# Output tiles summed in pairs from one pool of six PSUM banks, in place of groups of four from a pool of four banks

## The chip, the cores and the metric

The kernel runs on one core of one Trainium2 chip. The metric is the device time of one execution in microseconds (us); the median of several runs counts. The engines are named as in the profile: PE is TensorE (matmuls), PEld its weight loads, DVE is VectorE, ACT is ScalarE, POOL is GpSimd and SP is SyncE. A name with a q, such as SPq or ACTq, means what that engine issues for DMA.

## The reference, cut to what matters

One input `x` of 2048 tokens by 512 goes through two branches. Branch A is linear attention with 32 heads of 16, whose feature map is two softmaxes. Branch B is a gated MLP whose gate is mixed over the tokens. A sigmoid of `x` weighs the two.

```python
x = A_x
g = _sigmoid((x * gate_w).sum(-1, keepdims=True))
# branch A
qkv = (x @ wqkv).reshape(B, S, 3, H, Dh).transpose(2, 0, 3, 1, 4)
pq = einsum('bhsd,hdf->bhsf', q, w_phi)          # the same for k
phi_q = concatenate([softmax(pq), softmax(-pq)])  # the same for k
kv = einsum('bhsf,bhsd->bhfd', phi_k, v)
num = einsum('bhqf,bhfd->bhqd', phi_q, kv)
den = einsum('bhqf,bhf->bhq', phi_q, phi_k.sum(s)) + 1e-06
a = (num / den) @ wo
# branch B
z = gelu(x @ w_in)                       # 2048 x 1376
z1 = z[..., :688]
z2 = layernorm(z[..., 688:])
gate = einsum('ts,bsf->btf', w_sp, z2) + b_sp
b = (z1 * gate) @ w_out
return g * a + (1 - g) * b
```

## The kernel before

The 2048 tokens are 16 tiles of 128. The work has three stages.

The first stage (to about 46 us in the profile) computes `z1` and `z2` for all tiles (L188) and folds the feature weights into the projections of q and k (L308).

The second stage goes through the 16 tiles for the keys and values: `k_tile` and `v_tile` multiply a tile with its weights, and `kv_acc` sums the products in the PSUM tile `kvacc`. In between it already takes work of the third stage: `gg_next` calls `gg_half`, which makes one half of a tile's mixed gate with 16 matmuls of 128 by 344 (L449), and DVE turns the result into `ucat` (L454). After a tile's second half `u_T` has SP issue a DMA transpose of `ucat` into `uT` (L480). 16 of the 32 halves are done when this stage ends at about 120 us. `q_tile` (L357 for the matmuls, two exponentials on ACT at L361, then DVE, POOL and a DMA transpose into `eqT` at L391) has by then been called for six tiles.

The third stage, which the change is about, is the loop at L573. Three kinds of work alternate on PE:

- `attn_tile(i)`: eight small matmuls into the PSUM tile `at` (L462), which has one buffer; DVE makes `rden` and `o` of them (L465, L467), and SP issues the transpose of `o` into `oT` (L475).
- `q_tile(i + 6)` and `gg_next()`, as above.
- the output: `ba_main` sums nine matmuls of 128 by 512 for one tile, four with `oT` (L486) and five with `uT` (L488); `ba_rem` adds the last 48 rows of the 688 (L491); `ba_store` scales the sum on ACT into `ob` (L502) and ACT issues the store (L503). `ob` has two buffers.

The rows of `ba_rem` lie in the lower or the upper 64 partitions, depending on whether the tile is even or odd. `ba_step` sums one tile at each step of the loop and keeps the sums of a group of four (`BA_GROUPS`; the last group has two) in PSUM. At the group's last tile it does the four `ba_rem` matmuls one behind the other, and then the four stores. Tiles 14 and 15 are done by `ba_tile` at the end, with `ba_rem` over all 128 partitions; tile 15 is cut into columns 0 to 384 and 384 to 512, and the second piece goes out through DVE and SP (L498, L500).

PSUM has eight banks. `kvacc` and later `at` take two (tag `kvat`). In the second stage the other six are the pool `psK`. Ahead of the loop `psK` is closed and its six banks become `psG` with two buffers (for `q_tile` and `gg_half`) and `psC` with four (for the output sums).

The order of PE and ACT is the program's order (`manual_schedule`); DVE, POOL and SP are put in order by the scheduler. Each engine works its queue in order.

Of the kernel before, what the change touches and what calls it, by code (L numbers as in the profile page):

```python
# [10 lines left out]
FP32 = mybir.dt.float32  # L11
BF16 = mybir.dt.bfloat16
I32 = mybir.dt.int32

P = 128
S = 2048
D = 512
# [5 lines left out]
NT = S // P  # L23
NDT = D // P
CH = 512
NCH = S // CH
NFT = (FH + P - 1) // P
FPAD = NFT * P
NG = 4
# [6 lines left out]
def kernel(  # L36
# [43 lines left out]
    halves = [slice(64 * h, 64 * h + 64) for h in range(2)]  # L80
# [238 lines left out]
    with tc.manual_schedule(engines={mybir.EngineType.PE, mybir.EngineType.Activation}):  # L319
# [22 lines left out]
    early_cm.__exit__(None, None, None)  # L342
    psM = ctx.enter_context(
        tc.tile_pool(name="psM", bufs=1, space=bass.MemoryType.PSUM, reuse_waits="tile"))
    psK_cm = tc.tile_pool(name="psK", bufs=6, space=bass.MemoryType.PSUM, reuse_waits="tile")
    mm_pool = psK_cm.__enter__()
    work = ctx.enter_context(tc.tile_pool(name="work", bufs=2, reuse_waits="tile"))
    kvp_cm = tc.tile_pool(name="kvp", bufs=2, side="right", reuse_waits="tile")
    kvp = kvp_cm.__enter__()

    def mm_tile():
        return mm_pool.tile([P, CH], FP32, name="mm")

    def expo(pool, name, bufs, tt, w):
        ps = mm_tile()
        for dt in range(NDT):
            nc.tensor.matmul(ps[:, :], lhsT=xT[:, dt, tt * P:(tt + 1) * P], rhs=w[:, dt, :],  # L357
                             start=(dt == 0), stop=(dt == NDT - 1))
        e = pool.tile([P, H, 2, DH], BF16, name=name, bufs=bufs)
        for a in range(2):  # L360
            nc.scalar.activation(  # L361
                out=e[:, :, a, :], in_=ps[:, :].rearrange("p (h f) -> p h f", f=DH),
                func=AF.Exp, scale=1.0 - 2.0 * a)
        z = work.tile([P, H, 2], FP32, name="zs")
        nc.vector.tensor_reduce(  # L365
            out=z[:].rearrange("p h a -> p (h a)"), in_=e[:].rearrange("p h a f -> p (h a) f"),
            axis=AX.X, op=ALU.add,
        )
        return e, z

    def even_out(e, z, rz):
        ratio = work.tile([P, H], FP32, name="ratio")
        nc.vector.tensor_tensor(out=ratio[:], in0=z[:, :, 0], in1=rz, op=ALU.mult)  # L373
        nc.gpsimd.tensor_tensor(  # L374
            out=e[:, :, 1, :], in0=e[:, :, 1, :],
            in1=ratio[:, :, None].to_broadcast([P, H, DH]), op=ALU.mult)
# [8 lines left out]
    def q_tile(tt):  # L385
        eq, z = expo(work, "eq", 3, tt, wq_p)
        rq = work.tile([P, H], FP32, name="rq")
        nc.vector.reciprocal(out=rq[:], in_=z[:, :, 1])
        even_out(eq, z, rq[:])
        eqT = work.tile([P, 8, P], BF16, name="eqT", bufs=7)  # L390
        nc.sync.dma_start_transpose(out=eqT[:, :, :], in_=eq[:].rearrange("p h a f -> p (h a f)"))  # L391
        eqTs[tt] = eqT

# [65 lines left out]
    def attn_tile(tt):  # L459
        at = psM.tile([P, 8, P], FP32, name="at", tag="kvat", bufs=1)  # L460
        for g in range(8):
            nc.tensor.matmul(  # L462
                at[:, g, 0:AW], lhsT=eqTs[tt][:, g, :], rhs=kvz[:, g, :], start=True, stop=True)
        rden = work.tile([P, 8, NG], FP32, name="rden")
        nc.vector.reciprocal(out=rden[:], in_=at[:, :, 64:AW])  # L465
        o = work.tile([P, D], BF16, name="o")
        nc.vector.scalar_tensor_tensor(  # L467
            out=o[:].rearrange("p (u h d) -> p u h d", u=8, d=DH),
            in0=at[:, :, 0:64].rearrange("p u (h d) -> p u h d", d=DH),
            scalar=g_el[:, tt:tt + 1],  # L470
            in1=rden[:, :, :, None].to_broadcast([P, 8, NG, DH]),
            op0=ALU.mult, op1=ALU.mult,
        )
        oT = work.tile([P, NG, P], BF16, name="oT", bufs=5)
        nc.sync.dma_start_transpose(out=oT[:, :, :], in_=o[:, :])  # L475
        oTs[tt] = oT

    def u_T(tt):
        uT = work.tile([P, NFT, P], BF16, name="uT", bufs=11)
        nc.sync.dma_start_transpose(out=uT[:, :, :], in_=ucat[tt % NU][:, :])  # L480
        return uT

    def ba_main(acc, tt, c0=0, c1=D):
        oT, uT, i = oTs[tt], uTs[tt], tt % 2
        for g in range(NG):
            nc.tensor.matmul(acc, lhsT=oT[:, g, :], rhs=wo_t[:, g, c0:c1], start=(g == 0), stop=False)  # L486
        for ft in range(5):
            nc.tensor.matmul(acc, lhsT=uT[:, i + ft, :], rhs=w_main[i][:, ft, c0:c1], start=False, stop=False)  # L488

    def ba_rem(acc, tt, rows, c0=0, c1=D):  # L490
        nc.tensor.matmul(  # L491
            acc, lhsT=uTs[tt][rows, 5 * (1 - tt % 2), :], rhs=w_rem[rows, c0:c1], start=False, stop=True)

    def ba_store(acc, tt, c0, c1, on_dve):
        ob = work.tile([P, c1 - c0], BF16, name=f"ob{c1 - c0}")
        dst = out2[tt * P:(tt + 1) * P, c0:c1]
        if on_dve:
            nc.vector.tensor_scalar(  # L498
                out=ob[:, :], in0=acc, scalar1=g_inv[:, tt:tt + 1], scalar2=None, op0=ALU.mult)
            nc.sync.dma_start(out=dst, in_=ob[:, :])  # L500
        else:
            nc.scalar.activation(out=ob[:, :], in_=acc, func=AF.Copy, scale=g_inv[:, tt:tt + 1])  # L502
            nc.scalar.dma_start(out=dst, in_=ob[:, :])  # L503

    def acc_tile():
        return psC.tile([P, CH], FP32, name="acc")

    def ba_tile(tt, cuts=(0, D)):
        for h, (c0, c1) in enumerate(zip(cuts, cuts[1:])):
            acc = acc_tile()[:, 0:c1 - c0]  # L510
            ba_main(acc, tt, c0, c1)
            ba_rem(acc, tt, slice(0, P), c0, c1)
            ba_store(acc, tt, c0, c1, h > 0)

    def ba_step(tt):
        group = next(g for g in BA_GROUPS if tt in g)
        accs[tt] = acc_tile()
        ba_main(accs[tt][:, :], tt)
        if tt == group[-1]:
            for t in group:  # L520
                ba_rem(accs[t][:, :], t, halves[t % 2])
            for t in group:
                ba_store(accs[t][:, :], t, 0, D, False)

    oTs = {}
    uTs = {}
    eqTs = {}
    accs = {}
    BA_GROUPS = [range(0, 4), range(4, 8), range(8, 12), range(12, 14)]
    Q_AT = (5, 7, 9, 11, 13, 15)  # L530
    ggs = [(tt, j) for tt in range(NT) for j in range(2)]

    def gg_next():
        tt, j = ggs.pop(0)
        gg_half(tt, j)
        if j == 1:
            uTs[tt] = u_T(tt)

    with tc.manual_schedule(engines={mybir.EngineType.PE, mybir.EngineType.Activation}):
        ks = {0: k_tile(0)}  # L540
        kvacc = psM.tile([P, 8, P], FP32, name="kvacc", tag="kvat", bufs=1)
        pend = []
        for tt in range(NT):
            if tt + 1 < NT:
                ks[tt + 1] = k_tile(tt + 1)
            ek, rk = ks.pop(tt)
            pend.append((tt, ek, v_tile(tt, rk)))
            if len(pend) == 3:
                kv_acc(*pend.pop(0))
            if tt > 0:  # L550
                gg_next()
            if tt in Q_AT:
                q_tile(Q_AT.index(tt))
        nc.scalar.activation(out=g_el[:, :], in_=glog[:, :], func=AF.Exp)
        nc.vector.tensor_scalar(out=g_1p[:, :], in0=g_el[:, :], scalar1=1.0, scalar2=None, op0=ALU.add)
        nc.vector.reciprocal(out=g_inv[:, :], in_=g_1p[:, :])
        for p_ in pend:
            kv_acc(*p_)
        kvz_evac()
        kvp_cm.__exit__(None, None, None)  # L560
        kvw_cm.__exit__(None, None, None)
        outw = ctx.enter_context(
            tc.tile_pool(name="outw", bufs=1, side="right", reuse_waits="tile"))
        gg_next()
        w_main, w_rem, wo_t = load_out_weights()
        nq = len(Q_AT)
        psK_cm.__exit__(None, None, None)
        mm_pool = ctx.enter_context(
            tc.tile_pool(name="psG", bufs=2, space=bass.MemoryType.PSUM, reuse_waits="tile"))
        psC = ctx.enter_context(  # L570
            tc.tile_pool(name="psC", bufs=4, space=bass.MemoryType.PSUM, reuse_waits="tile"))
        attn_tile(0)
        for i in range(NT - 1):  # L573
            if i + nq < NT:
                q_tile(i + nq)
            gg_next()
            attn_tile(i + 1)
            if i == 0:
                gg_next()
            elif i < NT - 1:  # L580
                ba_step(i - 1)
        ba_tile(14)
        ba_tile(15, cuts=(0, 384, D))


# [28 lines left out]
```

## Time and profile before

| What | Value |
|---|---|
| median of 3 runs | 210.19 us (210.04 to 210.28) |
| the profiled execution | 210.28 us |
| its span, first to last instruction | 208.6 us |
| mean granted clock of PE | 0.997 |
| DVE busy | 131.2 us (63%) |
| ACT busy | 75.0 us (36%) |
| POOL busy | 47.0 us (23%) |
| L449, the halves of the gate | 512 matmuls, 79.9 us busy |
| L488 and L486, the output sums | 85 and 61 matmuls recorded, 20.1 and 15.6 us busy |
| L502, the stores' scaling on ACT | 16 instructions, 10.9 us busy |
| transposes into uT: issue to landing | 2.7 / 2.8 / 6.4 us (min, median, max of 16) |
| transposes into oT: issue to landing | 2.4 / 2.5 / 5.3 us (of 16) |

A matmul's duration in a row reaches from its start to its modelled end and overlaps the next one's, so what a run of matmuls costs is read from start to start: 16 of L449 take 2.33 us, four of L357 or L486 0.86 us, five of L488 1.08 us, eight of L462 0.26 us. Some matmul records are missing, which is why a count can be one too low.

### The profile page before, as it was taken

What the parts mean: (1) busy time and instruction counts of PE and PEld (TensorE: products, weight loads), DVE (VectorE), ACT (ScalarE), POOL (GpSimd) and SP (SyncE); (2) the same over time, 40 slices, a digit from 0 to 9 for tenths busy, and PEclk for the clock granted to TensorE, in tenths of its full rate; (3) what the DMA queues carried; (4) which work ended last, traced back from release to release, by engine and by line L of the source; (5) the groups of instructions that cost most, each with busy time, mean ns of one, the idle gap of its engine ahead of it and who ended that gap; (6) DMA issues with size and microseconds to landing.
All of it is one profiled execution on the core that took longest, in us unless ns stands there. A gap on an engine that the chain in (4) does not pass through costs nothing.

```text
span 208.6 us, 3745 instructions
## 1 busy us (share of the span) xinstructions
PE 202.5 (97%) x1432; PEld 121.5 (58%) x1449; DVE 131.2 (63%) x282; ACT 75.0 (36%) x121; POOL 47.0 (23%) x79
## 2 busy tenths in 40 slices
PE   8899999999999999999999999999999999999994
PEld 3566667665656565655556656555455555665642
DVE  2477786764996787979788667555448553443330
ACT  3566666668223423232323222222251123302322
POOL 8020202020544242424252322222204220110000
PEclk9999999999999999999999999999999999999998
DMA  6999999999920404224040599854562558264342
GB/s 187 269 219 211 216 286 155 269 270 207 290 58 0 42 2 88 51 40 83 9 88 0 97 339 164 152 91 88 106 157 57 111 107 137 75 113 89 105 113 75
DMA packets 88994, 27.20 MB, mean 130 GB/s; under 512 B 82992, under 2 KB 88976, under 8 KB 88976
## 3 DMA queue, kind: packets, MB, share of 16 engines
q1 hardware_dynamic: 83680, 22.42, 56.1%
q10 hardware_dynamic: 5232, 4.54, 7.4%
q8 instruction: 11, 0.18, 0.3%
q14 instruction: 7, 0.06, 0.1%
q0 software_dynamic: 64, 0.01, 0.0%
HBM read 4.41 MB, written 2.10 MB: 31 GB/s over the span
## 4 chain that ended last, share of the span: by engine, by line
PE 91%; DMA 4%; ACT 2%; issue 1%; DVE 0%; SPq 0%; ACTq 0%
PE mm L449 35%; PE zp L188 18%; PE mm L357 12%; PE acc L488 8%; PE mm L397 7%; PE acc L486 6%; DMA w_z<-in_B_w_in_dram 2%; PE kvacc L413 2%; PE at L462 2%; DMA out_dram<-ob 1%; PE acc L491 1%; ACT ob L502 1%; PE fps L308 1%; ACT eq L361 1%; ACTq L503 0%
## 5 line engine op out<-in xcount | busy, mean ns | idle before, releaser
L449 PE MATMUL mm<-z2all,wspT 128*128 128x344 bf16 x512 | 79.9, 309 | 0.6 <-DVE ucat L454 0.4
L449 PEld LDWEIGHTS <-wspT 128*128 128x128 bf16 x512 | 49.0, 98 | 26.3 <-issue 1.4
L188 PE MATMUL zp<-w_z,xT 128*128 128x344 bf16 (+1 forms) x256 | 40.2, 311 | 0.5 <-DMA w_z<-in_B_w_in_dram 0.3
L361 ACT ACTIVATE eq<-mm 128x512 bf16<-128x512 f32 x32 | 17.4, 594 | 53.0 <-PE mm L357 36.6
L365 DVE TENSOR_REDUCE zs<-eq 128x64 f32<-128x1024 bf16 x16 | 19.5, 1219 | 23.6 <-ACT eq L361 23.6
L188 PEld LDWEIGHTS <-xT 128*128 128x128 bf16 x256 | 24.5, 98 | 12.1 <-DVE xT L279 0.7
L454 DVE SCALAR_TENSOR_TENSOR ucat<-mm,bT,z1all 128x344 bf16<-128x344 f32 x32 | 17.4, 545 | 21.2 <-PE mm L449 21.2
L374 POOL TENSOR_TENSOR eq<-eq,ratio 128x512 bf16<-128x512 bf16 x16 | 16.9, 1059 | 52.5 <-DVE ratio L373 35.8
L361 ACT ACTIVATE ek<-mm 128x512 bf16<-128x512 f32 x32 | 17.2, 603 | 25.2 <-PE mm L357 25.2
L502 ACT ACTIVATE ob<-acc,g_inv 128x512 bf16<-128x512 f32 (+1 forms) x16 | 10.9, 680 | 33.9 <-PE acc L491 23.2
L365 DVE TENSOR_REDUCE zs<-ek 128x64 f32<-128x1024 bf16 x16 | 19.3, 1210 | 2.8 <-ACT ek L361 2.8
L488 PE MATMUL acc<-slabs,uT 128*128 128x512 bf16 (+2 forms) x85 | 20.1, 366 | 0.0
L357 PEld LDWEIGHTS <-xT 128*128 128x128 bf16 x128 | 12.3, 98 | 13.0 <-PE acc L491 0.8
L374 POOL TENSOR_TENSOR ek<-ek,ratio 128x512 bf16<-128x512 bf16 x16 | 16.9, 1059 | 2.2 <-DVE ratio L373 1.3
L357 PE MATMUL mm<-wq_p,xT 128*128 128x512 bf16 x62 | 16.3, 379 | 0.1
L397 PE MATMUL mm<-wv_sb,xT 128*128 128x512 bf16 x63 | 16.4, 379 | 0.1
L357 PE MATMUL mm<-wk_p,xT 128*128 128x512 bf16 x57 | 15.7, 379 | 0.4
L486 PE MATMUL acc<-slabs,oT 128*128 128x512 bf16 (+2 forms) x61 | 15.6, 365 | 0.4
L206 DVE BATCH_NORM_STATS2 bn<-z2all 128x6 f32<-128x344 bf16 x32 | 14.9, 503 | 0.0
L203 ACT ACTIVATE z2all<-zp 128x688 bf16<-128x688 f32 x16 | 11.9, 744 | 8.2 <-PE zp L188 7.8
L243 ACT ACTIVATE z1all<-zp 128x688 bf16<-128x688 f32 x16 | 11.9, 744 | 6.7 <-PE zp L188 6.7
L488 PEld LDWEIGHTS <-uT 128*128 128x128 bf16 x85 | 8.2, 98 | 9.2
(78 smaller groups left out, 149.0 us busy)
## 6 DMA issues: line engine op xcount, KB each, us to landing
out_dram<-ob ACTq DMA_DIRECT2D x15, 128.0 KB, 2.2
slabs<-in_B_w_out_dram ACTq DMA_DIRECT2D x2, 640.0 KB, 6.9
w_z<-in_B_w_in_dram SPq DMA_DIRECT2D x2, 344.0 KB, 4.7
w_z<-in_B_w_in_dram ACTq DMA_DIRECT2D x3, 172.0 KB, 3.4
wv_sb<-in_A_wqkv_dram SPq DMA_DIRECT2D x1, 512.0 KB, 4.4
slabs<-in_A_wo_dram ACTq DMA_DIRECT2D x1, 512.0 KB, 3.5
xs<-in_A_x_dram SPq DMA_DIRECT2D x2, 128.0 KB, 3.4
xs<-in_A_x_dram SPq DMA_DIRECT2D x1, 256.0 KB, 5.2
```

The lines of the kernel that those rows point to most:

```text
L188: nc.tensor.matmul(zp[:, j, 0:n], lhsT=xT[:, dt, tt * P:(tt + 1) * P], rhs=wt[:, dt, j * HF:j * HF + n], start=(dt == 0), stop=(dt == NDT ...
L206: nc.vector.bn_stats(out=bn6[:, tt, j, :], in_=z2v[:, j, :])
L357: nc.tensor.matmul(ps[:, :], lhsT=xT[:, dt, tt * P:(tt + 1) * P], rhs=w[:, dt, :], start=(dt == 0), stop=(dt == NDT - 1))
L361: nc.scalar.activation(out=e[:, :, a, :], in_=ps[:, :].rearrange("p (h f) -> p h f", f=DH), func=AF.Exp, scale=1.0 - 2.0 * a)
L365: nc.vector.tensor_reduce(out=z[:].rearrange("p h a -> p (h a)"), in_=e[:].rearrange("p h a f -> p (h a) f"), axis=AX.X, op=ALU.add,)
L374: nc.gpsimd.tensor_tensor(out=e[:, :, 1, :], in0=e[:, :, 1, :], in1=ratio[:, :, None].to_broadcast([P, H, DH]), op=ALU.mult)
L397: nc.tensor.matmul(v_ps[:, :], lhsT=xT[:, dt, tt * P:(tt + 1) * P], rhs=wv_sb[:, dt, :], start=(dt == 0), stop=(dt == NDT - 1))
L449: nc.tensor.matmul(gp[:, 0:HF], lhsT=wspT[:, st, tt * P:(tt + 1) * P], rhs=z2all[:, st, j * HF:(j + 1) * HF], start=(st == 0), stop=(st == ...
L454: nc.vector.scalar_tensor_tensor(out=ucat[tt % NU][:, c0 + j * HF:c0 + (j + 1) * HF], in0=gp[:, 0:HF], scalar=bT[:, tt:tt + 1], in1=z1all[ ...
L486: nc.tensor.matmul(acc, lhsT=oT[:, g, :], rhs=wo_t[:, g, c0:c1], start=(g == 0), stop=False)
L488: nc.tensor.matmul(acc, lhsT=uT[:, i + ft, :], rhs=w_main[i][:, ft, c0:c1], start=False, stop=False)
L502: nc.scalar.activation(out=ob[:, :], in_=acc, func=AF.Copy, scale=g_inv[:, tt:tt + 1])
```

## The change

The pools `psK`, `psG` and `psC` go. One tag `mm` with six buffers in `psM` serves `q_tile`, `gg_half` and the output sums, in the second stage as in the third. Three buffer counts change: `eqT` 7 to 8, `oT` 5 to 4, `uT` 11 to 9.

`ba_step` with its groups of four gives way to `ba_pair`, which does two tiles in one go: two `ba_main`, two `ba_rem`, two stores. It is called at every second step of the loop, from step 2 on.

The loop is put in another order. Before, a step is q, half of the gate, attention of the next tile, one output sum. After, a step is attention, q, half of the gate, and at even steps a pair. So the last half of the gate (of tile 15) stands behind the attention of tile 15 and behind the pair of tiles 12 and 13, directly ahead of `ba_tile(14)`. Tile 15 is cut into two equal halves of 256 columns.

```diff
-    psK_cm = tc.tile_pool(name="psK", bufs=6, space=bass.MemoryType.PSUM, reuse_waits="tile")
-    mm_pool = psK_cm.__enter__()
...
     def mm_tile():
-        return mm_pool.tile([P, CH], FP32, name="mm")
+        return psM.tile([P, CH], FP32, name="mm", tag="mm", bufs=6)
...
-        eqT = work.tile([P, 8, P], BF16, name="eqT", bufs=7)
+        eqT = work.tile([P, 8, P], BF16, name="eqT", bufs=8)
...
-        oT = work.tile([P, NG, P], BF16, name="oT", bufs=5)
+        oT = work.tile([P, NG, P], BF16, name="oT", bufs=4)
...
-        uT = work.tile([P, NFT, P], BF16, name="uT", bufs=11)
+        uT = work.tile([P, NFT, P], BF16, name="uT", bufs=9)
...
-    def ba_tile(tt, cuts=(0, D)):
-        for h, (c0, c1) in enumerate(zip(cuts, cuts[1:])):
-            acc = acc_tile()[:, 0:c1 - c0]
-            ba_main(acc, tt, c0, c1)
-            ba_rem(acc, tt, slice(0, P), c0, c1)
-            ba_store(acc, tt, c0, c1, h > 0)
-
-    def ba_step(tt):
-        group = next(g for g in BA_GROUPS if tt in g)
-        accs[tt] = acc_tile()
-        ba_main(accs[tt][:, :], tt)
-        if tt == group[-1]:
-            for t in group:
-                ba_rem(accs[t][:, :], t, halves[t % 2])
-            for t in group:
-                ba_store(accs[t][:, :], t, 0, D, False)
+    def ba_tile(tt, nsplit=1):
+        w = D // nsplit
+        for h in range(nsplit):
+            acc = mm_tile()
+            ba_main(acc[:, 0:w], tt, h * w, (h + 1) * w)
+            ba_rem(acc[:, 0:w], tt, slice(0, P), h * w, (h + 1) * w)
+            ba_store(acc[:, 0:w], tt, h * w, (h + 1) * w, h > 0)
+
+    def ba_pair(p):
+        accs = [mm_tile() for _ in range(2)]
+        for s_ in range(2):
+            ba_main(accs[s_][:, :], 2 * p + s_)
+        for s_ in range(2):
+            ba_rem(accs[s_][:, :], 2 * p + s_, halves[s_])
+        for s_ in range(2):
+            ba_store(accs[s_][:, :], 2 * p + s_, 0, D, False)
...
-        psK_cm.__exit__(None, None, None)
-        mm_pool = ctx.enter_context(
-            tc.tile_pool(name="psG", bufs=2, space=bass.MemoryType.PSUM, reuse_waits="tile"))
-        psC = ctx.enter_context(
-            tc.tile_pool(name="psC", bufs=4, space=bass.MemoryType.PSUM, reuse_waits="tile"))
-        attn_tile(0)
-        for i in range(NT - 1):
+        for i in range(NT):
+            attn_tile(i)
             if i + nq < NT:
                 q_tile(i + nq)
-            gg_next()
-            attn_tile(i + 1)
-            if i == 0:
+            if ggs:
                 gg_next()
-            elif i < NT - 1:
-                ba_step(i - 1)
+            if i >= 2 and i % 2 == 0:
+                ba_pair((i - 2) // 2)
         ba_tile(14)
-        ba_tile(15, cuts=(0, 384, D))
+        ba_tile(15, nsplit=2)
```

More of the change, by code (lines that the diff above doesn't have):

```diff
@@ L503, in ba_store @@
             nc.scalar.dma_start(out=dst, in_=ob[:, :])
-    def acc_tile():
-        return psC.tile([P, CH], FP32, name="acc")
-    def ba_tile(tt, cuts=(0, D)):
-        for h, (c0, c1) in enumerate(zip(cuts, cuts[1:])):
-            acc = acc_tile()[:, 0:c1 - c0]
-            ba_main(acc, tt, c0, c1)
-            ba_rem(acc, tt, slice(0, P), c0, c1)
-            ba_store(acc, tt, c0, c1, h > 0)
-    def ba_step(tt):
-        group = next(g for g in BA_GROUPS if tt in g)
-        accs[tt] = acc_tile()
-        ba_main(accs[tt][:, :], tt)
-        if tt == group[-1]:
-            for t in group:
-                ba_rem(accs[t][:, :], t, halves[t % 2])
-            for t in group:
-                ba_store(accs[t][:, :], t, 0, D, False)
+    def ba_tile(tt, nsplit=1):
[13 more added lines that the diff above has]
+            ba_store(accs[s_][:, :], 2 * p + s_, 0, D, False)
     oTs = {}
@@ L527 @@
     eqTs = {}
-    accs = {}
-    BA_GROUPS = [range(0, 4), range(4, 8), range(8, 12), range(12, 14)]
     Q_AT = (5, 7, 9, 11, 13, 15)
```

## The prediction

> **What bounds the kernel now.** I read the page first, then the chain of waits, then the timeline from the start of the loop at L573. The page:
>
> ```profile
> span 208.6 us, 3745 instructions
> PE 202.5 (97%) x1432; PEld 121.5 (58%) x1449; DVE 131.2 (63%) x282; ACT 75.0 (36%) x121; POOL 47.0 (23%) x79
> PE 91%; DMA 4%; ACT 2%; issue 1%; DVE 0%; SPq 0%; ACTq 0%
> ```
>
> PE sets the time; the other engines count only where PE waits for them. The changed program has the same 1449 weight loads and matmuls, of the same shapes but for tile 15's cut, and the same order of every engine up to the loop. So the question is what PE waits for inside the loop and at its end. The chain of waits from 118 to 160 us (start, length, what) shows the waits there are:
>
> ```profile
> 124.13 0.59 DVE ucat L454
> ...
> 124.76 2.49 PE mm L449 x16
> ...
> 154.75 1.09 ACT eq L361 x2
> 155.84 0.04 issue
> 155.88 2.49 PE mm L449 x16
> ```
>
> In both places a half of the gate waits for one of psG's two buffers. By starts: attention starts at 123.93 in the timeline and takes 0.26, so PE was free at 124.19 and began at 124.76: 0.57 us lost. The q matmuls start at 154.71 and take 0.86, so PE was free at 155.57 and began at 155.88: 0.31 lost. The second wait begins with the group of four stores: the third `ob` waits 1.41 us for the first store to land, and q's exponentials queue behind the stores on ACT. Every other step of the loop adds up start to start (2.33 + 0.26 + 0.86 + 1.08 + 0.86). Two more readings are needed, the remainder and the end (timeline; idle and releaser in brackets):
>
> ```profile
> 170.12 1.24 PE L488 MATMUL acc<-slabs,uT 128*128 128x512 bf16 x5
> 171.29 0.61 PE L491 MATMUL acc<-slabs,uT 64*128 64x512 bf16 x4
> 171.83 1.04 PE L357 MATMUL mm<-wq_p,xT 128*128 128x512 bf16 x4
> ...
> 199.46 1.24 PE L488 MATMUL acc<-slabs,uT 128*128 128x512 bf16 x5
> 200.63 0.39 PE L491 MATMUL acc<-slabs,uT 64*128 64x512 bf16 x2
> 200.95 1.04 PE L486 MATMUL acc<-slabs,oT 128*128 128x512 bf16 x4
> ```
>
> The five matmuls take 1.08, so four remainders cost 171.83 − 171.20 = 0.63 us, and two cost 200.95 − 200.54 = 0.41. Two more matmuls add only 0.22, about one 128x512 matmul (0.216): the two halves of the rows run side by side. The other 0.19 is paid once per visit.
>
> ```profile
> 198.34 0.42 PE L462 MATMUL at<-kvz,eqT 128*128 128x68 bf16 x8
> 198.54 0.57 DVE L454 SCALAR_TENSOR_TENSOR ucat<-mm,bT,z1all 128x344 bf16<-128x344 f32 x1 [2.90 <-PE mm L449]
> 199.14 1.21 SPq L480 DMA_TRANSPOSE uT<-ucat  x1
> ...
> 205.51 0.35 DVE L498 TENSOR_SCALAR ob<-acc,g_inv 128x128 bf16<-128x128 f32 x1 [5.34 <-PE acc L491]
> 205.88 0.36 SPq L500 DMA_DIRECT2D out_dram<-ob  x1
> ```
>
> The landing is that of this transpose. Asked for the transpose at 199.14 alone, the tile view answers:
>
> ```profile
> DMA to landing us min/median/max: 2.8/2.8/2.8
> ```
>
> The last half of the gate ends at 198.34, where the next matmul starts; `uT` of tile 15 lands at 199.14 + 2.8 = 201.94. PE wants it at 203.77. In between stand attention 15, tile 13, a remainder pair, tile 14 and the `oT` part of tile 15: 5.43 us of cover for a path of 3.60.
>
> **The change, part by part.**
>
> *One pool of six buffers:* both waits go, −0.57 and −0.31. A buffer comes round after six tiles. In the busiest stretch that is one period of two steps: 2 × (0.26 + 0.86 + 2.33) + 2 × 1.94 + 0.41 = 11.2 us. What must empty it is late by at most the two stores ahead of q's exponentials, some 2.3 us (149.19 to 151.05, plus a gap of 0.46), and the exponentials' own 1.09. So I put the new wait at nothing; without that cover it would be about 1 us per pair. DVE's new order puts two reductions of 1.22 ahead of `ucat` and `o` once, at the loop's start; `o` of tile 2 is then done near 131 and attention 3 wants `at` near 135. The group's store wait of 1.41 to 2.94 goes too, as two `ob` serve two stores. The smaller `oT`, `uT` and larger `eqT` counts fit: `oT` of tile 4 needs tile 0's pair, which is done two steps earlier. All at 0; bounds −0.1 and +0.9, a second stall as long as the two lost ones.
>
> *Pairs:* seven visits instead of three of four and one of two: 7 × 0.41 − (3 × 0.63 + 0.41) = 2.87 − 2.30 = +0.57. Bounds: −0.76 if a pair costs one matmul's 0.22, +0.7.
>
> The Trainium skill, "TensorEngine Tiling (Array Packing)", Key Properties, says that a change of the tiling mode drains TensorE; it gives no duration. By that page's speedup of up to 2× alone the term would be 0, and the sum below +0.45; by the rows, which contain the drain, it is +0.57 and +1.02.
>
> *The last half of the gate, moved to the end:* this adds a wait. Behind it come only tile 14 (ten matmuls, 2.16 us) and the first four of tile 15 (256 wide: between 0.163 for 384 and 0.066 for 128, so 0.11 each, 0.44). Cover 2.60. The path is as before, 0.20 + 0.57 + 0.03 + 2.8 = 3.60. Wait 1.00, and a weight load of 0.10 that is no longer hidden: +1.10. Behind the waiting load on PE stand the 16 last matmuls, and behind these both last scalings and stores; nothing covers them. SP's queue is passed in another order: `oT` of tile 15 now stands ahead of `uT` of tile 15, but attention 15 now precedes the half by 2.6 us; `o` is done about 1.0 us before the half's end, its issue takes 1.2, and SP is free 0.6 before `uT` comes. Bounds: 0.5 (a landing of 2.2, below the shortest of 16, 2.7) and 3.4 (transposes issued 1.1 to 1.3 us ahead of a group's stores landed after 4.5 to 4.9 instead of 2.4 to 3.2, so up to 2.3 more). I take 1.10: here the pair's stores are issued some 2.8 and 1.6 us ahead of the transpose, like the `oT` at 154.4 behind stores at 153.15 and 154.31, which landed in 2.5.
>
> The Trainium skill, "DMA: Bandwidth & Descriptors", Rules for kernel authors, speaks against this move: issue a DMA early and wait late, so that its fixed cost overlaps. With the same page's fit for another issuing path (about 2.0 us plus bytes over 436 GB/s, Anatomy of one DMA) an estimate for 192 KB is 2.45, the wait 0.75 and the sum +0.67; the rows say 2.8.
>
> *Tile 15 in equal halves:* PE about equal (20 × 0.11 against 1.63 + 0.66). The last scaling is 256 wide: 0.35 at 128 and 0.57 at 344 (L454) give 0.48, +0.13. The last store is 64 KB: between 1.5 us (32 KB) and 1.7 (96 KB), +0.10.
>
> Sum: −0.88 + 0.57 + 1.10 + 0.23 = **+1.02 us**, so the profiled execution goes from 210.28 to 211.3 and its span from 208.6 to 209.6. The median is 0.09 below that execution: 210.19 + 1.02 = **211.2**.
>
> **The rivals.**
>
> *A: the landing is hidden.* `uT` of tile 15 comes before PE wants it, and the freed waits pay for the rest: −0.88 + 0.57 + 0.23 = −0.08, 210.1. For: SP is idle then and no store is issued during the first 2 us. Against: it needs a landing of 1.8, and even 2.2 leaves 0.5 of wait; the shortest of 16 was 2.7. From 2.2 down the result is within the noise. Chance 0.09.
>
> *B: a pair's remainder costs no switch,* as attention's short weight loads may slip in: 7 × 0.22 − 2.30 = −0.76, sum −0.31, 209.9. Against: both sizes of group show the 0.19, ahead of different successors. Chance 0.06.
>
> *C: the last transpose collides with the stores* of tiles 12 and 13: +2.3 at most, 211.8 to 213.5. For: the 4.5 to 4.9 above. Chance 0.10.
>
> *D: the pool does not do what it says:* stalls of the old size come back in the loop, from the stores on ACT or from DVE's order: +0.9, 212.1. Against: PE's instructions ask for the buffer of six tiles earlier. Chance 0.12.
>
> **How the numbers follow.** The forecast has 0.63, its own range 210.8 to 211.7 (landing 2.7 to 3.1, pair 0.36 to 0.43). No change means within 0.2%, 209.77 to 210.61, about what a measurement can tell: most of A and half of B, 0.11. Faster: the rest of B and a tail of A with a cheaper pair, 0.04. Slower 0.85. For 8 in 10 the range takes in D, the nearer half of C and the dear half of A: 210.4 to 212.4.
>
> **What would show it.** In the chain, no DVE `ucat` wait near 124 and no ACT wait near 156; seven remainder pairs of 0.41 each, start to start; a PE wait of about 1 us on DMA `uT` ahead of the last 16 matmuls; the last scaling at 0.48. The prediction is wrong if that wait is under 0.5 or over 1.6, or if new PE waits stand within the loop.

## The result, and the profile after

The changed kernel takes 211.22 us in the median of 4 runs (210.79 to 211.54), the kernel before 210.24 us (210.04 to 210.44, 4 runs). The ratio is 1.0045, with a 95% interval of 1.0025 to 1.0066: slower by 0.98 us. By the bound of 2% that is no difference; by the kernel's own scatter it is one. The profiled execution took 211.54 us, 1.26 more than that of the kernel before; of this 0.26 lies ahead of the loop, whose first attention starts at 120.74 instead of 120.48. The page of the changed kernel:

```profile
span 209.8 us, 3742 instructions
PE 203.4 (97%) x1430; PEld 121.4 (58%) x1449; DVE 131.4 (63%) x282; ACT 74.9 (36%) x121; POOL 46.9 (22%) x79
PE 93%; DMA 4%; issue 1%; SPq 1%; DVE 1%
```

Nothing in it tells where the time went; PE is busy for 97% in both. The waits say more. From 118 us to the end, this is the whole list of PE's waits (who, on whom, us in total, times, longest):

```profile
PE mm L486 <- DMA uT<-ucat: 0.7, 1, 0.7
```

The same list of the kernel before has one wait, on DVE's `ucat`; it is not there, and there is a new one on a transpose. (The shorter stall near 156 is too short for this list, and so is one of 0.15 at the end.) The timeline of PE at the place of the stall near 124, and behind the pair of tiles 2 and 3, where a q follows two stores:

```profile
124.19 0.42 PE L460 MATMUL at<-kvz,eqT 128*128 128x68 bf16 x8
124.45 1.02 PE L355 MATMUL mm<-wq_p,xT 128*128 128x512 bf16 x4
125.31 2.50 PE L447 MATMUL mm<-z2all,wspT 128*128 128x344 bf16 x16
...
146.88 1.02 PE L355 MATMUL mm<-wq_p,xT 128*128 128x512 bf16 x4
147.74 2.50 PE L447 MATMUL mm<-z2all,wspT 128*128 128x344 bf16 x16
```

From start to start these are 0.26, 0.86 and again 0.86, the plain lengths. All starts of the loop add up like this, up to the end. One pair of output tiles, with what follows it:

```profile
133.90 1.24 PE L486 MATMUL mm<-slabs,uT 128*128 128x512 bf16 x5
135.08 0.39 PE L489 MATMUL mm<-slabs,uT 64*128 64x512 bf16 x2
135.40 0.43 PE L460 MATMUL at<-kvz,eqT 128*128 128x68 bf16 x8
```

The five matmuls take 1.08, so the remainders cost 135.40 − 134.98 = 0.42, and so in each of the seven pairs, to 0.01. The end, in the timeline (idle time before an instruction and what ended it in brackets):

```profile
200.04 1.19 SPq L473 DMA_TRANSPOSE oT<-o  x1
...
200.97 1.03 PE L484 MATMUL mm<-slabs,oT 128*128 128x512 bf16 x4
201.17 0.58 DVE L452 SCALAR_TENSOR_TENSOR ucat<-mm,bT,z1all 128x344 bf16<-128x344 f32 x1 [1.19 <-PE mm L447]
...
201.77 1.21 SPq L478 DMA_TRANSPOSE uT<-ucat  x1
...
203.27 0.33 PEld L484 LDWEIGHTS <-oT 128*128 128x128 bf16 x4 [0.48 <-DMA oT<-o]
...
204.59 0.72 PE L486 MATMUL mm<-slabs,uT 128*128 128x256 bf16 x5 [0.71 <-DMA uT<-ucat]
...
206.55 0.48 DVE L496 TENSOR_SCALAR ob<-mm,g_inv 128x256 bf16<-128x256 f32 x1 [4.81 <-PE mm L489]
...
207.06 0.36 SPq L498 DMA_DIRECT2D out_dram<-ob  x1
```

Tile 14 starts at 200.97 and takes 2.16, so PE wanted `oT` of tile 15 at 203.13 and had it at 203.28: 0.15 lost. The four matmuls with it take 0.44, so PE wanted `uT` at 203.72 and went on at 204.59: 0.87 lost. Together 1.02. The two are not independent: with `oT` in time PE would have stood at `uT` from 203.57, and still until 204.59. So the whole 1.02 is the wait for `uT`, which landed at 201.77 + 2.77 = 204.54.

For the comparisons below I use one measure beside the run times: the loop, from the start of attention 0 on PE to the start of the last scaling on DVE. It leaves out the first two stages, whose order none of the kernels changes (but for the half named below the table) and whose end scatters between profiled executions, from 119.91 us in e3 to 122.58 in e1. In the profiled executions of e1 and e8 the granted clock was 0.91 for the first 20 us, where it was 1.00 in the others, so their loops start some 2 us later and their own times (213.25 and 212.37 us) tell nothing of the loop, in which their clock was 1.00 as well.

| kernel | loop, us | last scaling to end of span | median time, us | ratio to before (95%) |
|---|---|---|---|---|
| before | 85.03 | 3.06 | 210.24 | |
| changed | 85.81 | 3.24 | 211.22 | 1.0045 (1.0025 to 1.0066) |
| e1 loop order undone | 85.72 | 3.23 | 211.39 | 1.0054 (1.0027 to 1.0081) |
| e2 last half early | 87.19 | 3.23 | 213.39 | 1.0125 (1.0095 to 1.0156) |
| e3 before, in pairs | 85.34 | 3.06 | 210.62 | 1.0013 (0.9990 to 1.0037) |
| e4 full rows | 86.05 | 3.25 | 211.53 | 1.0057 (1.0033 to 1.0082) |
| e5 before, half early | 84.45 | 3.05 | 209.62 | 0.9951 (0.9916 to 0.9986) |
| e6 before, half late | 87.81 | 3.06 | 213.10 | 1.0107 (1.0072 to 1.0141) |
| e7 before, four ob | 84.71 | 3.05 | 210.10 | 0.9963 (0.9931 to 0.9994) |
| e8 before, both | 85.17 | 3.08 | 209.76 | 0.9939 (0.9901 to 0.9976) |

The kernel before had a median of 210.34 us beside e1 to e4 and of 210.59 beside e5 to e8. In e5 and e8 one half of the gate more lies ahead of attention 0; its 2.33 us are added to the loop. The loop is read from one execution of each kernel, the times from all runs.

### The profile page after: what moved, and what is told of

It reads as the page before. It is cut to its first block, busy times and chain, and to the rows that moved or that the text cites. A ratio compares the mean times of both kernels' runs of the same rounds, so it can differ in the third digit from the quotient of the medians.

```text
span 209.8 us, 3742 instructions
## 1 busy us (share of the span) xinstructions
PE 203.4 (97%) x1430; PEld 121.4 (58%) x1449; DVE 131.4 (63%) x282; ACT 74.9 (36%) x121; POOL 46.9 (22%) x79
## 4 chain that ended last, share of the span: by engine, by line
PE 93%; DMA 4%; issue 1%; SPq 1%; DVE 1%
PE mm L447 36%; PE zp L188 17%; PE mm L355 13%; PE mm L486 8%; PE mm L395 7%; PE mm L484 6%; DMA xs<-in_A_x_dram 3%; PE at L460 2%; PE kvacc L411 2%; DMA uT<-ucat 1%; PE mm L489 1%; PE fps L308 1%; PE tp L273 0%; DVE ucat L452 0%; DVE ob L496 0%
## 5 line engine op out<-in xcount | busy, mean ns | idle before, releaser
L188 PEld LDWEIGHTS <-xT 128*128 128x128 bf16 x256 | 24.5, 98 | 11.8 <-DVE xT L279 0.7
L500 ACT ACTIVATE ob<-mm,g_inv 128x512 bf16<-128x512 f32 (+1 forms) x16 | 10.8, 674 | 51.2 <-PE mm L489 47.6
L452 DVE SCALAR_TENSOR_TENSOR ucat<-mm,bT,z1all 128x344 bf16<-128x344 f32 x32 | 18.0, 563 | 8.3 <-PE mm L447 8.3
L486 PE MATMUL mm<-slabs,uT 128*128 128x512 bf16 (+1 forms) x82 | 19.9, 366 | 0.9 <-DMA uT<-ucat 0.7
L463 DVE RECIPROCAL rden<-at 128x32 f32<-128x32 f32 x16 | 5.4, 339 | 22.4 <-PE at L460 22.4
L355 PEld LDWEIGHTS <-xT 128*128 128x128 bf16 x128 | 11.8, 97 | 10.8 <-issue 0.2
L484 PE MATMUL mm<-slabs,oT 128*128 128x512 bf16 (+1 forms) x65 | 16.0, 366 | 0.2
L355 PE MATMUL mm<-wq_p,xT 128*128 128x512 bf16 x59 | 15.6, 378 | 0.2
```

The lines of the kernel that those rows point to most:

```text
L188: nc.tensor.matmul(zp[:, j, 0:n], lhsT=xT[:, dt, tt * P:(tt + 1) * P], rhs=wt[:, dt, j * HF:j * HF + n], start=(dt == 0), stop=(dt == NDT ...
L452: nc.vector.scalar_tensor_tensor(out=ucat[tt % NU][:, c0 + j * HF:c0 + (j + 1) * HF], in0=gp[:, 0:HF], scalar=bT[:, tt:tt + 1], in1=z1all[ ...
```

## The experiments

**e1: the changed kernel in the old loop order.** Pool and pairs are kept, and `uT` gets a tenth buffer. The edit to the loop:

```diff
-        for i in range(NT):
-            attn_tile(i)
+        attn_tile(0)
+        for i in range(NT - 1):
             if i + nq < NT:
                 q_tile(i + nq)
-            if ggs:
+            gg_next()
+            attn_tile(i + 1)
+            if i == 0:
                 gg_next()
-            if i >= 2 and i % 2 == 0:
+            elif i % 2 == 0:
                 ba_pair((i - 2) // 2)
```

> The changed kernel with the loop order of before (two halves of the gate at step 0, the next tile's attention ahead of the pair), one pool and pairs kept; uT gets a tenth buffer for it. My theory: the two waits at the end (0.15 us on oT and 0.87 us on uT of tile 15, 1.02 together) go, the rest stays: 211.2 - 1.0 = 210.2 us, and PE has no DMA wait at the end. Rival: the time is lost in the pairs and the single pool, wherever the last half stands: still 211.2.

Measured: 211.39 us, so by the time alone the rival wins. The trace says otherwise. The end is free of waits: from the start of tile 14 to the last scaling it takes 203.75 to 208.30, 4.55 us, against 200.97 to 206.55, 5.58, in the changed kernel, which is the 1.02 of the theory. But a stall came up in the middle. The timeline of e1 there:

```profile
175.99 1.08 ACT L359 ACTIVATE eq<-mm 128x512 bf16<-128x512 f32 x2 [0.49 <-ACT ob L500]
...
177.11 1.22 DVE L363 TENSOR_REDUCE zs<-eq 128x64 f32<-128x1024 bf16 x1 [5.08 <-ACT eq L359]
...
179.32 0.75 DVE L465 SCALAR_TENSOR_TENSOR o<-at,g_el,rden 128x512 bf16<-128x512 f32 x1
...
180.22 0.41 PE L460 MATMUL at<-kvz,eqT 128*128 128x68 bf16 x8 [0.71 <-DVE o L465]
```

The last q's exponentials run behind the pair's two stores on ACT, DVE has its reduction of them queued ahead of `o`, and the next attention wants `at`, which has one buffer, only 2.6 us after the last. PE's starts lose 0.87 here. 85.81 − 1.02 + 0.87 = 85.66, against 85.72 measured: the loop is accounted for to 0.06. The expected time was missed since undoing the order was no clean undoing: it met a wait of the kind that the prediction had as rival D. The changed kernel's own order, attention ahead of q, doesn't have it.

**e2: only the last half of the gate earlier.** The edit to the loop of the changed kernel (`uT` gets a tenth buffer here too):

```diff
             if ggs:
                 gg_next()
+            if i == 0:
+                gg_next()
```

> The changed kernel with one edit of its order only: two halves of the gate at step 0, so the last half is done a step earlier; attention 15 stays directly ahead of tile 14 (uT gets a tenth buffer). My theory: what counts at the end is the cover of whatever transpose comes last. uT is early now, but oT of tile 15 has only attention 15 and tile 14 as cover (0.27 + 2.16 = 2.4 us) for 1.67 us to its issue plus 2.4 to 3.2 us to landing: a wait of 1.6 to 2.4 us on oT in place of 1.0, so 211.8 to 212.6. Rival, uT alone was late: 210.2.

Measured: 213.39 us, loop 87.19. The end of e2 in the timeline:

```profile
200.93 0.43 PE L460 MATMUL at<-kvz,eqT 128*128 128x68 bf16 x8
...
202.61 1.19 SPq L473 DMA_TRANSPOSE oT<-o  x1
...
203.14 0.38 PE L489 MATMUL mm<-slabs,uT 128*128 128x512 bf16 x1
...
205.77 0.61 PE L484 MATMUL mm<-slabs,oT 128*128 128x256 bf16 x4 [2.25 <-DMA oT<-o]
```

`uT` is in time now, and PE waits for `oT` instead, and longer: 205.77 − 203.36 = 2.41 us from start to start. 85.81 − 1.02 + 2.41 = 87.20: the loop to 0.01. The wait is at the dear end of what was expected, as `oT` took 3.12 us to land; it was issued at 202.61, between the two stores of the pair (201.75 and 202.91). The time is 0.8 us over the expected range. A later start of the loop, 120.97 against 120.74, is 0.23 of it in the profiled execution; the rest is not explained. The rival falls. What the last half pays for is the length of PE work behind the last transpose, whichever that is.

**e3: the kernel before in pairs.**

```diff
-    BA_GROUPS = [range(0, 4), range(4, 8), range(8, 12), range(12, 14)]
+    BA_GROUPS = [range(t, t + 2) for t in range(0, 14, 2)]
```

> The kernel before with groups of two in place of groups of four, nothing else. My theory: seven visits of 0.41 us replace three of 0.63 and one of 0.41, +0.57; the store waits of a group of four go and with them the 0.31 us stall near 156: 210.24 + 0.26 = 210.5. Rival, a visit has no fixed cost (0.22 per pair): 210.24 - 0.76 - 0.31 = 209.2.

Measured: 210.62 us, ratio 1.0013 (0.9990 to 1.0037), loop +0.31 where +0.26 was expected. The stall near 156 is gone from the starts, 154.34 to 155.20 being the plain 0.86; the one near 124 is still there at 0.58:

```profile
124.19 2.49 PE L449 MATMUL mm<-z2all,wspT 128*128 128x344 bf16 x16 [0.41 <-DVE ucat L454]
...
154.34 1.03 PE L357 MATMUL mm<-wq_p,xT 128*128 128x512 bf16 x3
155.20 2.50 PE L449 MATMUL mm<-z2all,wspT 128*128 128x344 bf16 x16
```

The interval of the times holds no change too, but not the rival's 209.2.

**e4: full rows in the pairs.** The remainders of the changed kernel's pairs run over all 128 partitions, the rest being zeros:

```diff
-            ba_rem(accs[s_][:, :], 2 * p + s_, halves[s_])
+            ba_rem(accs[s_][:, :], 2 * p + s_, slice(0, P))
```

> The changed kernel with the remainders of the pairs over all 128 rows (zeros in the rest), as tiles 14 and 15 have them: no half-row matmuls side by side, but twice 0.216 = 0.43 us per pair. If a visit's fixed cost belongs to the half-row form and lies all inside the 0.42 us that the pairs took start to start: 7 x 0.01, no change, 211.2 to 211.3. If part of it lies in what follows (attention behind a pair took 0.27 instead of 0.26): slightly less, 211.1. Rival, half rows cost nothing beyond their matmuls: 211.2 + 7 x 0.21 = 212.7.

Measured: 211.53 us. One pair in the timeline of e4:

```profile
133.42 1.24 PE L486 MATMUL mm<-slabs,uT 128*128 128x512 bf16 x5
134.50 0.59 PE L489 MATMUL mm<-slabs,uT 128*128 128x512 bf16 x2
134.93 0.42 PE L460 MATMUL at<-kvz,eqT 128*128 128x68 bf16 x8
```

Here the two remainders follow one another, 134.93 − 134.50 = 0.43. A whole period of two steps takes 11.23 (130.60 to 141.83, starts of L484) against 11.22 with half rows (131.09 to 142.31). So in a pair the half rows gain nothing: what running side by side saves, 0.216, the visit's fixed 0.19 to 0.20 eats. In a group of four they do gain, 0.63 against four times 0.216. The loop is 0.24 longer than the changed kernel's; 0.22 of it stands at one place that the edit doesn't touch, the first output sum at 130.60, which in this execution waited for the first `oT` (landed at 130.55).

**e5: the kernel before, the extra half ahead of the loop.**

```diff
         gg_next()
+        gg_next()
         w_main, w_rem, wo_t = load_out_weights()
...
-            if i == 0:
-                gg_next()
-            elif i < NT - 1:
+            if i > 0:
                 ba_step(i - 1)
```

> The kernel before with the loop's extra half of the gate moved ahead of the loop, behind the half that stands there, so that it runs in the six-buffer pool. My theory: the 0.57 us stall of L449 near 124 goes, nothing else: 210.24 - 0.57 = 209.7. Rival, the stall moves (the new pool's first tiles wait for the old one's to be emptied): 210.2.

Measured: 209.62 us, ratio 0.9951 (0.9916 to 0.9986): faster than the kernel before, and so than the changed one. The place of the stall:

```profile
122.73 0.42 PE L462 MATMUL at<-kvz,eqT 128*128 128x68 bf16 x8
122.99 1.02 PE L357 MATMUL mm<-wq_p,xT 128*128 128x512 bf16 x4
123.85 2.50 PE L449 MATMUL mm<-z2all,wspT 128*128 128x344 bf16 x16
```

The loop is 0.58 shorter, and PE's list of waits from 118 us on is empty (the stall near 156 is still there, 0.30 from start to start). The theory's 0.57 holds.

**e6: the kernel before, the last half at the end.**

```diff
-            if i == 0:
-                gg_next()
-            elif i < NT - 1:
+            if i > 0:
                 ba_step(i - 1)
+        gg_next()
         ba_tile(14)
```

> The kernel before with the extra half left out at step 0 and the last half directly ahead of tile 14, groups of four, pools and the uneven cut kept. My theory: the 0.57 us stall near 124 goes, and at the end uT of tile 15 has tile 14 and four matmuls of 384 as cover (2.16 + 0.65) for 3.60 us plus a weight load of 0.10: a wait of 0.9. 210.24 - 0.57 + 0.9 = 210.6. Rival A, the landing is hidden: 209.7.

Measured: 213.10 us, 2.5 more than expected. Two lines of e6's timeline tell why, and a third what was right:

```profile
125.33 4.39 SPq L475 DMA_TRANSPOSE oT<-o  x2
...
130.47 1.04 PE L486 MATMUL acc<-slabs,oT 128*128 128x512 bf16 x4 [1.69 <-DMA oT<-o]
...
206.95 0.99 PE L488 MATMUL acc<-slabs,uT 128*128 128x384 bf16 x5 [0.62 <-DMA uT<-ucat]
```

At the end, 206.95 − 206.17 = 0.78 is lost, where 0.9 was expected: in the old kernel too, with its groups, pools and uneven cut, the late half costs about what it costs in the changed one, less the 0.21 by which four matmuls of 384 are longer than four of 256. But the half left out at the start had been the cover of the first `oT`. That transpose is issued at 125.33 (the row joins it with the next one), takes 3.1 us to issue and 5.1 to land, and PE loses 1.85 on it. And the 0.57 near 124 didn't go: the q that now follows the first half waits for its `ucat`. 85.03 + 0.78 + 1.85, and 0.14 more at the stall near 156, make 87.80; measured are 87.81.

**e7: the kernel before, four buffers for the stores' tile.**

```diff
-        ob = work.tile([P, c1 - c0], BF16, name=f"ob{c1 - c0}")
+        ob = work.tile([P, c1 - c0], BF16, name=f"ob{c1 - c0}", bufs=4 if c1 - c0 == D else 1)
```

> The kernel before with four buffers for the 512-wide ob (the two small ones get one each, for room). My theory: the third and fourth store of a group no longer wait for the first two to land (1.4 to 2.9 us), q's exponentials come earlier, and the 0.31 us stall near 156 goes: 209.9. Rival, the stall belongs to psG and stays: 210.2.

Measured: 210.10 us, ratio 0.9963 (0.9931 to 0.9994), loop −0.32. The exponentials behind the first group start at 153.88 instead of 154.75, and the half behind q starts 0.86 after it: the stall near 156 is gone, as the theory had it.

```profile
153.88 1.09 ACT L361 ACTIVATE eq<-mm 128x512 bf16<-128x512 f32 x2 [0.47 <-ACT ob L502]
154.86 1.03 PE L357 MATMUL mm<-wq_p,xT 128*128 128x512 bf16 x4
155.72 2.50 PE L449 MATMUL mm<-z2all,wspT 128*128 128x344 bf16 x16
```

**e8: e5 and e7 together.**

> The kernel before with both edits, the extra half ahead of the loop and four ob buffers. My theory: both stalls go, 0.88 us: 209.4, faster than both kernels, with the groups of four and the long cover at the end kept. Rival, the stalls hide each other or return elsewhere: 209.7 to 210.2.

Measured: 209.76 us, ratio 0.9939 (0.9901 to 0.9976). It is faster than both kernels, but it misses the 209.4 that was expected, and that it is faster than e5 can't be told. Its profiled execution shows where the gain can go:

```profile
131.64 0.42 PE L462 MATMUL at<-kvz,eqT 128*128 128x68 bf16 x8
132.92 1.04 PE L486 MATMUL acc<-slabs,oT 128*128 128x512 bf16 x4 [0.86 <-DMA oT<-o]
```

Both stalls are gone, but PE loses 132.92 − 131.90 = 1.02 on the first `oT`: 85.03 − 0.88 + 1.02 = 85.17, the loop as measured. That is one execution, in which the loads of the output weights ended late (below); how much of it the others lose isn't shown.

## Why the prediction was right

The prediction said 211.2 with a range of 210.4 to 212.4; 211.22 was measured, +0.98 against +1.02. In the two profiled executions the loop is 0.78 longer and what follows it 0.18, together +0.96. The mechanism held, term by term; that the sum is met this closely has some luck in it, since the terms were off by +0.07, −0.08 and −0.05. Step by step:

- *One pool of six buffers, −0.88.* Right. No gap is left in the loop at either place. e5 removes the first stall alone (−0.58) and e7 the second alone (−0.32), in the kernel before. One point of the reading stays open: near 124 the half waits for DVE to empty the half directly before it (`ucat`, 124.13 to 124.72), although the q ahead of that one had left its buffer at 122.94 (ACT's exponentials, 121.85 to 122.94). In e6 a q in that place waits in the same way, and in e5, where psG serves q, half and q in the same order, it doesn't. That one pool has no such stall is shown; how psG's two buffers were handed out isn't.
- *Seven pairs, +0.57.* Right: 0.42 for each of the seven, so 7 × 0.42 − 2.30 = +0.64, and e3 puts the pairs alone at +0.31 with one stall gone, thus 0.62 for the visits. Rival B, no fixed cost, falls; e4 shows how dear that cost is, since full rows are as fast. That it is a change of mode is not shown here, only the cost. The Trainium skill, "TensorEngine Tiling (Array Packing)", Key Properties, would fit, as it has a change of tiling mode drain TensorE; the speedup of up to 2× that the page has under Theoretical Speedup isn't met by a pair (0.42 against 0.43).
- *The last half at the end, +1.10.* Right in kind and nearly in size (1.02). The path of `uT` was as worked out: 200.97 to 201.77 and 2.77 to land; PE went on 0.05 after that, where 0.10 was put for the weight load. One thing was missed, and it cost nothing: I had `oT` of tile 15 in time, but it landed 3.18 us after its issue, and PE stood 0.15 for it ahead of the longer wait. In the changed kernel the seven `oT` issued between the two stores of a pair took 3.1 to 4.5 us, and of the eight others behind the first, seven took 2.4 to 2.5 (the one at 155.38 took 4.0). Rival A falls with the wait, rival C with the landing of 2.77. The Trainium skill's rule for this, in "DMA: Bandwidth & Descriptors", Rules for kernel authors (issue early, wait late), agrees with the loss; the estimate of 2.45 us from that page was 0.3 short of the 2.77 measured. e2 shows that the cover and not the half itself is what counts, e6 that the wait belongs to the order and not to the pool or the pairs.
- *The cut in equal halves, +0.23.* The scaling was right, 0.48 in place of 0.35. The last store's +0.10 was over: from its issue to the end of the span 2.73 us against 2.68, so +0.05, and +0.18 in all.
- *Rival D, new stalls in the loop.* Not in the changed kernel, whose loop of 85.81 is −0.88 + 0.64 + 1.02 from 85.03. e1 shows that it was no idle thought: with the old order and the new pairs there is one, 0.87 us, from the very queue named, q's exponentials behind the stores.

The weakness of the prediction lies elsewhere: it took the start of the loop as safe. The first `oT` lands within 0.2 us of its use before (125.05 + 5.30 = 130.35, used at 130.55), and the runs show 0.22 us lost there in the profiled execution of e4, 1.02 in that of e8 and 1.85 in that of e6. That of the changed kernel had some 0.5 us to spare (125.27 + 5.25 = 130.52, used at 131.09).

What stays open: the version that would keep the one pool and drop the waits at the end, with attention 15 and the last half ahead of the last pair, has no measured time, nor has one that takes e7's buffers with another q ahead of the extra half. The expectations written down for them, 210.2 and 209.4 us, are untested.

## What to carry to other kernels

At the end of a kernel, count the PE work behind each last transfer: its issue, its landing and the engine ahead of it must fit in, and when one is moved, the next one becomes the last (`oT` for `uT` in e2). The work that is moved was cover somewhere: the half that is put at the end here was at the start the cover of the first `oT`. The matmuls on half the rows paid a fixed cost per visit here, 0.19 to 0.20 us, so they are worth gathering: in fours they gain (0.63 against 0.86), in pairs full rows with zeros do as well.

## What the runs showed of the hardware that was not expected

A transpose that is issued while the output weights are being loaded lands only when these have landed. ACT issues the five loads (1.9 MB) just ahead of the loop, and in all ten profiled executions the first `oT` landed 1.7 to 1.9 us after the last of them: 128.42 and 130.35 in the kernel before, 127.42 and 129.32 in e5, 131.18 and 132.87 in e8. So its landing took 3.9 to 5.6 us from the issue, where 2.4 to 2.5 is usual away from loads and stores, and its issue held SP for 1.9 to 3.4 us where 1.2 is usual. The end of the loads scatters by 1.75 us between the executions (from the start of attention 0, put 2.33 earlier as in the table, 7.0 us in e5 and 8.8 in e8; the order on SP is the same in both), and with it the room at the first output sum: 0.5 us to spare in e5, 1.02 lost in e8. What in the DMA makes it so isn't shown.

Two half-row matmuls of 64 by 512 side by side, with the fixed cost of the visit, take 0.42 us, as long as two of the full 128 rows one after the other (0.43).
